# ScalarE takes the first tap of a convolution, and one w_out slice is converted in the fourth stage in place of the second

## The chip, the cores and the metric

One core of a Trainium2 chip runs the kernel. The metric is the device time of one execution in microseconds (us). TensorE (PE) does the matmuls, VectorE (DVE), ScalarE (ACT) and GpSimdE (POOL) the elementwise work, SyncE (SP) issues the transfers. Every engine works off its own queue in order, so an instruction that waits holds up all that stands behind it on that engine.

## The reference, cut to what matters

Causal attention with 2 x 12 heads over 448 tokens, then two feed-forward blocks on 896 tokens of width 768. The second block is where the convolution stands:

```python
h = np.maximum(x @ w_in, 0.0)                 # 768 -> 1024
conv_out = np.zeros_like(h)
for k in range(3):                            # along the tokens
    conv_out += conv_w[k][None, None, :] * hp[:, k:k + S, :]
gate = 1.0 / (1.0 + np.exp(-conv_out))
return (h * gate @ w_out).astype(np.float32)  # 1024 -> 768
```

## The kernel before, in words

Five stages follow each other, and TensorE works in all of them. The first is attention and the receptance products with `w_r`. The second multiplies by `w_k` (slices `wk0` to `wk7`, PSUM tiles `pk`), the third by `w_v` (`wv0` to `wv5`, `pv`), the fourth by `w_in` (`wi0` to `wi7`, `ph`), the fifth by `w_out` (`pout`). Every product of f32 numbers is three matmuls (L64, L65, L66): each operand is split into a high part and a remainder, the low part. L64 and L65 need only the high part of the weight, L66 the low part.

The weights lie in memory as 64-bit floats, and each slice is converted before TensorE can use it. One conversion is a transfer into one of two `wraw` buffers (issued by SP, L122), a ScalarE instruction L100 on the raw words, four VectorE instructions L102, L104, L106 and L108, the split of the high part on ScalarE (L74) and that of the low part on VectorE (L78). The second raw read, L108, frees the `wraw` buffer for the transfer after the next. Tiles `wc` have two buffers; the split weights `whl` have three. The eight slices of `w_out` (`wo0` to `wo7`) are converted ahead of the fifth stage, between the conversions of the other weights: the list `wo_after` says behind which slice each is loaded (two slices later), and calls of `convert_next()` in the loops say where it is converted. Before, three stand in the second stage, three in the third, and two at the end of the fourth.

In the fourth stage, for each of eight slices f and both halves b of the tokens: ScalarE takes the maximum with zero out of PSUM into `hT` (L595), which frees the PSUM bank. VectorE makes the three taps of the convolution in a tile `cv` (L597 multiplies by the first weight, L598 and L599 add the others). ScalarE does the sigmoid (L602), GpSimdE multiplies with `hT` (L603), ScalarE and VectorE split the product into `g` (L74, L78). `hT` has two buffers (one per f), the pool of `cv` three (one per f and b). The PSUM banks are used in a ring of eight, so the first six output tiles `pout` take the banks of `ph4`, `ph5` and `ph6`.

From the second stage on a scheduler of the compiler orders the instructions of each engine by its own estimate of times.

Of the kernel before, what the change touches and what calls it, by code (L numbers as in the profile page):

```python
# [13 lines left out]
AF = mybir.ActivationFunctionType  # L14
ALU = mybir.AluOpType
# [4 lines left out]
def kernel(  # L20
# [18 lines left out]
    nc = tc.nc  # L39
    B, H, S, D = q.shape  # L40
# [9 lines left out]
    NF = DFF // P  # L50
    NE = DM // P
# [8 lines left out]
    def f32(ap):  # L60
        return ap.bitcast(F32)
# [6 lines left out]
    def split_h(eng, out_, in_):  # L68
        if eng == "p":
            nc.gpsimd.tensor_scalar(out_, in_, 1.0, 1.0, ALU.mult, ALU.mult)  # L70
        elif eng == "v":
            nc.vector.tensor_copy(out_, in_)
        else:
            nc.scalar.activation(out_, in_, AF.Copy)  # L74

    def split_l(eng, out_, x, h):
        e = nc.gpsimd if eng == "p" else nc.vector
        e.tensor_tensor(out_, x, f32(h), ALU.subtract)  # L78
# [76 lines left out]
    cw = const.tile([P, 3 * NF], F32, name="cw")  # L155
# [32 lines left out]
    def big(tag, name):  # L188
        return (act if tag in early else act2).tile([P, 2, NT], F32R, tag=tag, name=name)
# [173 lines left out]
    def token_mm(name, w, x, late):  # L363

        n = len(x)
        out_ = [bank(f"{name}_{b}") for b in range(B)]
        for c, b in sorted(((c, b) for b in range(B) for c in range(n)), key=lambda k: (late and k[0] == n - 1, k[1])):
            products(out_[b], w, x, b, n, c)
        return out_
# [8 lines left out]
    units = [(w_r, e, "wr", False) for e in range(NE)] + [(w_k, f, "wk", False) for f in range(NF)]  # L378
    units += [(w_v, e, "wv", False) for e in range(NE)] + [(w_in, f, "wi", False) for f in range(NF)]

    wo_after = [NE + f for f in (1, 3, 5)] + [NE + NF + e for e in (1, 3, 5)] + [len(units) - 1] * 2
    AHEAD = 2
    plan = []
    for u in range(len(units) + AHEAD):
# [24 lines left out]
    def step():  # L409

        if not running:
            running.append(steps_next())
        if next(running[0], running) is running:
            running.clear()

    def convert_next():
        step()
        while running:
            step()

    def take():

        while loaded and not loaded[0][0] and len(ready) <= AHEAD:
            convert_next()
        return ready.pop(0)
# [131 lines left out]
    for f in range(NF):  # L557
        w = take()
        k2.append(big(f"Y{f}", f"k2_{f}"))
        for b, pk in enumerate(token_mm(f"pk{f}", w, xk, f == 0)):  # L560
            t = TOK[b]
            a = mixp.tile([P, S], F32, tag="m", name=f"a{f}_{b}")
            nc.scalar.activation(a, pk, AF.Relu)
            nc.scalar.activation(a, a, AF.Square)
            split_h("s", k2[f][:, 0, t], a)
            split_l("v", k2[f][:, 1, t], a, k2[f][:, 0, t])
        if f in (1, 3, 5):
            convert_next()

    x2 = []  # L570
    for e in range(NE):
# [3 lines left out]
        for b, pv in enumerate(token_mm(f"pv{e}", w, k2, e == 0)):  # L575
            t = TOK[b]
            a = mixp.tile([P, S], F32, tag="m", name=f"xv{e}_{b}")
# [9 lines left out]
    for f in range(NF):  # L587
        w = take()
        g.append(big(f"Y{f}", f"g{f}"))
        hT = hp_.tile([P, B, S + 2], F32, tag="hT", name=f"hT{f}")  # L590
        nc.gpsimd.memset(hT[:, :, 0:S + 2:S + 1], 0.0)
        for b, ph in enumerate(token_mm(f"ph{f}", w, x2, f == 0)):
            t = TOK[b]
            hc = hT[:, b, 1:S + 1]
            nc.scalar.activation(hc, ph, AF.Relu)  # L595
            a = mixp.tile([P, S], F32, tag="m", name=f"cv{f}_{b}")
            nc.vector.tensor_scalar(a, hT[:, b, 0:S], cw[:, f:f + 1], None, ALU.mult)  # L597
            nc.vector.scalar_tensor_tensor(a, hc, cw[:, NF + f:NF + f + 1], a, ALU.mult, ALU.add)  # L598
            nc.vector.scalar_tensor_tensor(  # L599
                a, hT[:, b, 2:S + 2], cw[:, 2 * NF + f:2 * NF + f + 1], a, ALU.mult, ALU.add  # L600
            )
            nc.scalar.activation(a, a, AF.Sigmoid)  # L602
            nc.gpsimd.tensor_tensor(a, a, hc, ALU.mult)  # L603
            split_h("s", g[f][:, 0, t], a)
            split_l("v", g[f][:, 1, t], a, g[f][:, 0, t])
        if f == NF - 1:
            convert_next()
            convert_next()
# [56 lines left out]
```

## Time and profile before

| What | Value |
|---|---|
| Median of 3 runs | 393.79 us (392.92 to 394.78) |
| The profiled execution | 392.92 us, of it 391.1 us span |
| TensorE busy | 382.4 us (98% of the span) |
| VectorE busy | 302.1 us (77%) |
| ScalarE busy | 233.5 us (60%) |
| GpSimdE busy | 113.3 us (29%) |

The page divides the span into forty equal slices. VectorE is at 90% or more in the slices from about 275 to 340 us, which is the fourth stage, and TensorE nearly everywhere. A busy TensorE says little on whether it lost time: its starts do. In the second stage one matmul of 448 columns starts 0.21 us after the one before it, in the third and fourth 0.20 us, and one of 384 columns in the fifth 0.18 us. Where two starts stand farther apart than that, TensorE waited, also where the busy time of two matmuls hides it.

### The profile page before, as it was taken

To read this page: it belongs to the slowest core of one execution; us is meant where nothing else is said; L and a number is where in the kernel's file an instruction comes from. 1 tells how busy PE (TensorE), PEld (TensorE's weight loads), DVE (VectorE), ACT (ScalarE), POOL (GpSimd) and SP (SyncE) were. 2 spreads that over 40 slices of the span, in tenths; PEclk is the share of its full clock that TensorE was granted. 3 is DMA by queue.
4 is the path that set the end of the run, shared out by engine and by line. 5 is a ranking of instruction groups with operands and counts; after the bars stand their busy time and mean duration, and the time that the engine had idled before them with its cause. 6 is when DMAs were issued, how large, how long until landed. Compare 5 with 4: busy or idle time off the path is not lost.

```text
span 391.1 us, 6524 instructions
## 1 busy us (share of the span) xinstructions
PE 382.4 (98%) x2308; PEld 335.9 (86%) x2308; DVE 302.1 (77%) x622; ACT 233.5 (60%) x510; POOL 113.3 (29%) x165
## 2 busy tenths in 40 slices
PE   8999999999999999999998999999999999999996
PEld 7867767767879999898997999999999998999995
DVE  2689999998657886888988898988999999950000
ACT  3698999999426764878776564553545454432111
POOL 1258899999941000000000000000144142320000
PEclk9999999999999999999999999999999999999999
DMA  7546644512220332244554535344522220003111
GB/s 167 119 96 176 158 100 111 153 25 84 80 82 0 117 126 80 92 151 155 168 191 134 189 111 184 92 154 157 164 77 86 80 80 3 1 2 141 40 62 40
DMA packets 60156, 41.34 MB, mean 106 GB/s; under 512 B 34232, under 2 KB 59100, under 8 KB 60124
## 3 DMA queue, kind: packets, MB, share of 16 engines
q1 hardware_dynamic: 60124, 40.93, 34.8%
q8 instruction: 18, 0.29, 0.3%
q14 instruction: 14, 0.11, 0.1%
HBM read 38.17 MB, written 2.75 MB: 105 GB/s over the span
## 4 chain that ended last, share of the span: by engine, by line
PE 53%; DVE 16%; DMA 14%; ACT 7%; issue 7%; POOL 2%; ACTq 0%; SPq 0%; POOLq 0%; DVEq 0%
PE sc L251 7%; PE pp L290 7%; PE po L307 6%; PE pout L64 5%; PE pout L65 5%; PE pout L66 5%; PE pr L64 4%; PE pr L65 4%; PE pr L66 4%; PE warm L447 3%; PE ptrk L231 2%; DMA wk4raw<-in_moe_w_k_dram 1%; POOL cv L603 1%; DVE cv L598 1%; PE ptrq L231 1%
## 5 line engine op out<-in xcount | busy, mean ns | idle before, releaser
L603 POOL TENSOR_TENSOR cv<-cv,hT 128x448 f32<-128x448 f32 x16 | 24.2, 1515 | 204.2 <-ACT cv L602 202.4
L282 POOL TENSOR_SCALAR p<-p,st 112x112 f32<-112x112 f32 (+1 forms) x96 | 56.2, 603 | 21.6 <-DVE st L278 20.9
L270 ACT ACTIVATE p<-s,st 112x112 f32<-112x112 f32 (+3 forms) x96 | 50.5, 533 | 3.7 <-DVE st L262 3.6
L262 DVE CUSTOM_DVE_ANT_0 s<-sc,maskw 112x112 f32<-112x112 f32 (+3 forms) x96 | 39.3, 438 | 5.4 <-PE sc L251 3.0
L251 PE MATMUL sc<-kT,qT 64*112 64x112 f32 (+3 forms) x288 | 30.3, 324 | 0.0
L290 PEld LDWEIGHTS pp<-ident,p 112*112 112x112 f32 x240 | 23.1, 133 | 7.0 <-issue 3.0
L290 PE MATMUL pp<-ident,p 112*112 112x112 f32 x240 | 28.3, 264 | 0.7 <-DVE pt L298 0.7
L630 ACT ACTIVATE osb<-pout 128x384 f32<-128x384 f32 x14 | 6.8, 491 | 32.1 <-PE pout L66 32.0
L307 PE MATMUL po<-pt,rv 112*64 112x448 f32 (+3 forms) x192 | 25.3, 406 | 0.0
L251 PEld LDWEIGHTS sc<-kT,qT 64*112 64x112 f32 x288 | 19.1, 172 | 6.0 <-DVE st L278 0.3
L298 ACT COPY pt<-pp 112x448 f32<-112x448 f32 x36 | 19.1, 533 | 7.9 <-PE pp L290 7.8
L307 PEld LDWEIGHTS po<-pt,rv 112*64 112x64 f32 x192 | 12.7, 136 | 12.2 <-issue 5.5
L343 DVE SCALAR_TENSOR_TENSOR m<-xT,mu,m 128x448 f32<-128x448 f32 x24 | 17.3, 723 | 5.9 <-ACT m L339 3.0
L270 ACT ACTIVATION_READ_ACCUMULATOR p<-s,st 112x1 f32 x96 | 19.3, 201 | 0.0
L74 ACT ACTIVATE g<-cv 128x448 fp32r<-128x448 f32 x16 | 9.2, 576 | 15.7 <-POOL cv L603 15.7
L64 PE MATMUL pout<-wo_t,g 128*128 128x384 f32 x49 | 16.5, 338 | 0.9 <-ACT hT L595 0.9
L65 PE MATMUL pout<-wo_t,g 128*128 128x384 f32 x49 | 16.5, 336 | 0.0
L66 PE MATMUL pout<-wo_t,g 128*128 128x384 f32 x49 | 16.5, 336 | 0.0
L78 POOL TENSOR_TENSOR xr<-m,xr 128x448 fp32r<-128x448 f32 x12 | 16.1, 1341 | 1.0
L602 ACT ACTIVATE cv<-cv 128x448 f32<-128x448 f32 x16 | 9.3, 579 | 10.6 <-DVE cv L599 10.6
L65 PE MATMUL pout<-wo_u,g 128*128 128x384 f32 x42 | 14.1, 336 | 0.0
L64 PE MATMUL pout<-wo_u,g 128*128 128x384 f32 x42 | 14.1, 335 | 0.0
(501 smaller groups left out, 1199.9 us busy)
## 6 DMA issues: line engine op xcount, KB each, us to landing
rq<-in_q_dram SPq DMA_DIRECT2D x24, 112.0 KB, 2.8
rk<-in_k_dram SPq DMA_DIRECT2D x24, 112.0 KB, 2.8
rv<-in_v_dram SPq DMA_DIRECT2D x24, 112.0 KB, 2.8
out_dram<-osb SPq DMA_DIRECT2D x14, 192.0 KB, 1.9
wv0raw<-in_moe_w_v_dram SPq DMA_DIRECT2D x1, 1024.0 KB
wv1raw<-in_moe_w_v_dram SPq DMA_DIRECT2D x1, 1024.0 KB, 4.9
wv2raw<-in_moe_w_v_dram SPq DMA_DIRECT2D x1, 1024.0 KB, 4.9
wv3raw<-in_moe_w_v_dram SPq DMA_DIRECT2D x1, 1024.0 KB, 4.9
```

The costliest lines, as they stand in the source:

```text
L64: nc.tensor.matmul(ps_out, lh, rh, start=first, stop=False)
L65: nc.tensor.matmul(ps_out, lh, rl, start=False, stop=False)
L66: nc.tensor.matmul(ps_out, ll, rh, start=False, stop=last)
L251: nc.tensor.matmul(scs[j][:CP, :w], qT[r, 1 if pi == 2 else 0, c * CP:(c + 1) * CP], kT[r, 1 if pi == 1 else 0, :w], start=pi == 0, stop=p ...
L262: nc.vector.tensor_tensor_reduce(s_sb[:, :w], self.scs[c][j][:CP, :w], maskw[:, S - w:], -SCALE, 3e38, ALU.add, ALU.min, self.st[:, 0, i:i ...
L270: nc.scalar.activation(p, self.s[c, j][:, :w], AF.Exp, bias=self.st[:, 0, i:i + 1], scale=-1.0, accum_out=self.st[:, 1, i:i + 1],)
L282: nc.gpsimd.tensor_scalar(self.p[j, c], self.p[j, c], self.st[:, 2, i:i + 1], 1.0, ALU.mult, ALU.mult)
L290: nc.tensor.transpose(pp[:CP, i * CP:(i + 1) * CP], self.p[j, c][:, kc * CP:(kc + 1) * CP], ident[:CP, :CP])
L298: (nc.vector.tensor_copy if bi in TURN_V else nc.scalar.copy)(pt, self.pp[bi][:CP, :S])
L307: nc.tensor.matmul(self.po[j * D:(j + 1) * D, c0 * CP:S], self.raw["v"][:, kc, j], pt[:, off:off + S - c0 * CP], start=kc == 0, stop=self. ...
L343: nc.vector.scalar_tensor_tensor(m, xT[c][:, b, 1:S + 1], mu[:, a:a + 1], m, ALU.mult, ALU.add)
L603: nc.gpsimd.tensor_tensor(a, a, hc, ALU.mult)
```

## The change

L597, the first tap, is a ScalarE instruction with the weight as its scale in place of a VectorE multiplication. In the second stage `convert_next()` is called after f = 2 and f = 5 in place of 1, 3 and 5; in the fourth it is called once more after f = 3. The list `wo_after` follows: `wo0` is loaded behind `wk4` in place of `wk3`, `wo1` behind `wk7`, and `wo5` behind `wi5`. The third stage converts `wo2` to `wo4` in place of `wo3` to `wo5`.

```diff
-    wo_after = [NE + f for f in (1, 3, 5)] + [NE + NF + e for e in (1, 3, 5)] + [len(units) - 1] * 2
+    wo_after = [NE + f for f in (2, 5)] + [NE + NF + e for e in (1, 3, 5)] + [2 * NE + NF + 3] + [len(units) - 1] * 2
...
-        if f in (1, 3, 5):
+        if f in (2, 5):
             convert_next()
...
             a = mixp.tile([P, S], F32, tag="m", name=f"cv{f}_{b}")
-            nc.vector.tensor_scalar(a, hT[:, b, 0:S], cw[:, f:f + 1], None, ALU.mult)
+            nc.scalar.activation(a, hT[:, b, 0:S], AF.Copy, scale=cw[:, f:f + 1])
...
             split_l("v", g[f][:, 1, t], a, g[f][:, 0, t])
+        if f == 3:
+            convert_next()
         if f == NF - 1:
             convert_next()
             convert_next()
```

On SP, which issues the loads of the weights, this stood in the second stage before:

```order
L122 DMA wk3raw_2394<-in_moe_w_k_dram 128x6x128
L122 DMA wo0raw_2458<-in_moe2_w_out_dram 128x768
L122 DMA wk4raw_2518<-in_moe_w_k_dram 128x6x128
L122 DMA wk5raw_2530<-in_moe_w_k_dram 128x6x128
L122 DMA wo1raw_2590<-in_moe2_w_out_dram 128x768
L122 DMA wk6raw_2650<-in_moe_w_k_dram 128x6x128
L122 DMA wk7raw_2662<-in_moe_w_k_dram 128x6x128
L122 DMA wo2raw_2722<-in_moe2_w_out_dram 128x768
L122 DMA wv0raw_2782<-in_moe_w_v_dram 128x8x128
```

And now, at the same place:

```order
L122 DMA wk3raw_2394<-in_moe_w_k_dram 128x6x128
L122 DMA wk4raw_2458<-in_moe_w_k_dram 128x6x128
L122 DMA wo0raw_2518<-in_moe2_w_out_dram 128x768
L122 DMA wk5raw_2578<-in_moe_w_k_dram 128x6x128
L122 DMA wk6raw_2590<-in_moe_w_k_dram 128x6x128
L122 DMA wk7raw_2650<-in_moe_w_k_dram 128x6x128
L122 DMA wo1raw_2710<-in_moe2_w_out_dram 128x768
L122 DMA wv0raw_2770<-in_moe_w_v_dram 128x8x128
```

`wk4` stands ahead of `wo0`, and one slice fewer stands ahead of `wk6`, `wk7` and `wv0`.

On ScalarE, in the fourth stage around the two tiles `hT6` (`g` are the split products, `wo` slices of w_out), before:

```order
L602 ACTIVATE cv4_1_3727<-cv4_1_3727 128x448
L74 ACTIVATE g4_3676<-cv4_1_3727 128x448
L595 ACTIVATE hT6_3806<-ph6_0_3808 128x448
L595 ACTIVATE hT6_3806<-ph6_1_3809 128x448
L602 ACTIVATE cv5_0_3788<-cv5_0_3788 128x448
```

And now:

```order
L602 ACTIVATE cv4_1_3727<-cv4_1_3727 128x448
L597 ACTIVATE cv5_1_3797<-hT5_3747,cw_81 128x448
L74 ACTIVATE g4_3676<-cv4_1_3727 128x448
L595 ACTIVATE hT6_3806<-ph6_0_3808 128x448
L602 ACTIVATE cv5_0_3788<-cv5_0_3788 128x448
L74 ACTIVATE wo_u5_3357<-wo6c_3925 128x384
L74 ACTIVATE wo6hl_3933<-wo6c_3925 128x384
L74 ACTIVATE g5_3746<-cv5_0_3788 128x448
L597 ACTIVATE cv6_0_3847<-hT6_3806,cw_81 128x448
L602 ACTIVATE cv5_1_3797<-cv5_1_3797 128x448
L595 ACTIVATE hT6_3806<-ph6_1_3809 128x448
```

The taps stand between the others, and the second half of `hT6` now comes six instructions behind the first, after the sigmoid of `cv5_1`.

On VectorE, in the fourth stage ahead of the low part of `wi6`, before:

```order
L599 SCALAR_TENSOR_TENSOR cv2_1_3587<-hT2_3537,cw_81,cv2_1_3587 128x448
L102 TENSOR_SCALAR wi7c_3737<-wi7c_3737 128x768
L78 TENSOR_TENSOR g2_3536<-cv2_0_3578,g2_3536 128x448
L108 SCALAR_TENSOR_TENSOR wi6c_3667<-wi6raw_3595,wi6c_3667 128x768
L597 TENSOR_SCALAR cv3_0_3648<-hT3_3607,cw_81 128x448
L104 TENSOR_SCALAR wi7c_3737<-wi7c_3737 128x768
L597 TENSOR_SCALAR cv3_1_3657<-hT3_3607,cw_81 128x448
L598 SCALAR_TENSOR_TENSOR cv3_0_3648<-hT3_3607,cw_81,cv3_0_3648 128x448
L78 TENSOR_TENSOR g2_3536<-cv2_1_3587,g2_3536 128x448
L106 SCALAR_TENSOR_TENSOR wi7c_3737<-wi7raw_3665,wi7c_3737 128x768
L598 SCALAR_TENSOR_TENSOR cv3_1_3657<-hT3_3607,cw_81,cv3_1_3657 128x448
L78 TENSOR_TENSOR wi6hl_3673<-wi6c_3667,wi6hl_3673 128x768
```

And now:

```order
L599 SCALAR_TENSOR_TENSOR cv3_0_3636<-hT3_3595,cw_81,cv3_0_3636 128x448
L106 SCALAR_TENSOR_TENSOR wi6c_3667<-wi6raw_3653,wi6c_3667 128x768
L598 SCALAR_TENSOR_TENSOR cv3_1_3645<-hT3_3595,cw_81,cv3_1_3645 128x448
L104 TENSOR_SCALAR wi7c_3737<-wi7c_3737 128x768
L78 TENSOR_TENSOR g2_3524<-cv2_1_3575,g2_3524 128x448
L108 SCALAR_TENSOR_TENSOR wi6c_3667<-wi6raw_3653,wi6c_3667 128x768
L599 SCALAR_TENSOR_TENSOR cv3_1_3645<-hT3_3595,cw_81,cv3_1_3645 128x448
L106 SCALAR_TENSOR_TENSOR wi7c_3737<-wi7raw_3665,wi7c_3737 128x768
L78 TENSOR_TENSOR g3_3594<-cv3_0_3636,g3_3594 128x448
L598 SCALAR_TENSOR_TENSOR cv4_0_3718<-hT4_3677,cw_81,cv4_0_3718 128x448
L78 TENSOR_TENSOR wi6hl_3673<-wi6c_3667,wi6hl_3673 128x768
```

No L597 stands there any more, and the convolution is some three tap instructions further when the low part of `wi6` is made. From the first L598 of the stage to `wi6hl` there are 45 VectorE instructions now, among them all of the conversion of `wo5`.

## Rows read from the trace of the kernel before

**Rows 1.** Busy time by engine in the fourth stage and the start of the fifth.

```profile
core 0: us, PE busy (x) PEld busy (x) DVE busy (x) ACT busy (x) POOL busy (x), PEclk, DMA share, GB/s
276.00:349.60 73.60, 72.65 (x375) 68.57 (x374) 71.42 (x100) 35.58 (x63) 25.20 (x22) 1.00 0.20 65
```

**Rows 2.** Timeline of TensorE (start us, us, what) where wk4 begins.

```profile
178.40 0.36 PE L66 MATMUL pk<-xk,wk3hl 128*128 128x448 f32 x1
178.90 0.47 PE L64 MATMUL pk<-xk,wk4hl 128*128 128x448 f32 x1
```

**Rows 3.** Timeline of TensorE where the third stage begins.

```profile
208.72 0.37 PE L66 MATMUL pk<-xk,wk7hl 128*128 128x448 f32 x1
210.07 0.47 PE L64 MATMUL pv<-k,wv0hl 128*128 128x448 f32 x1 [0.99 <-ACT wv0hl L74]
...
210.80 0.37 PE L65 MATMUL pv<-k,wv0hl 128*128 128x448 f32 x1
211.33 0.47 PE L66 MATMUL pv<-k,wv0hl 128*128 128x448 f32 x1 [0.17 <-DVE wv0hl L78]
```

**Rows 4.** Timeline of TensorE in the first output tiles of the fifth stage.

```profile
329.31 0.34 PE L66 MATMUL pout<-wo_t,g 128*128 128x384 f32 x1
330.60 0.44 PE L64 MATMUL pout<-wo_t,g 128*128 128x384 f32 x1 [0.95 <-ACT hT L595]
```

**Rows 5.** Timeline of ScalarE at the same place: both halves of hT6.

```profile
330.02 0.96 ACT L595 ACTIVATE hT<-ph 128x448 f32<-128x448 f32 x2
```

**Rows 6.** Timeline of ScalarE, conversions in the second stage.

```profile
169.72 0.89 ACT L100 ACTIVATE wk4c<-wk4raw 128x768 f32<-128x768 f32 x1 [1.33 <-DMA wk4raw<-in_moe_w_k_dram]
...
196.49 0.89 ACT L100 ACTIVATE wo2c<-wo2raw 128x768 f32<-128x768 f32 x1 [1.70 <-DMA wo2raw<-in_moe_w_out_dram]
...
201.39 1.17 ACT L100 ACTIVATE wv0c<-wv0raw 128x1024 f32<-128x1024 f32 x1 [0.69 <-DMA wv0raw<-in_moe_w_v_dram]
...
208.98 1.04 ACT L74 ACTIVATE wv0hl<-wv0c 128x1024 fp32r<-128x1024 f32 x1
```

**Rows 7.** Lines L597 and L339: durations in ns, minimum/median/maximum, first and last start.

```profile
L597 DVE TENSOR_SCALAR cv<-hT,cw x16: 437/442/1333, 278.2 to 343.3; 128x448 f32<-128x448 f32 x16
L339 ACT ACTIVATE m<-xT,mu x12: 653/659/686, 119.0 to 150.1; 128x448 f32<-128x448 f32 x12
```

**Rows 8.** Timeline of VectorE in the fourth stage up to the low part of wi6.

```profile
307.63 0.55 DVE L104 TENSOR_SCALAR wi7c<-wi7c 128x768 int32<-128x768 int32 x1
308.10 0.44 DVE L597 TENSOR_SCALAR cv<-hT,cw 128x448 f32<-128x448 f32 x1
308.46 0.67 DVE L598 SCALAR_TENSOR_TENSOR cv<-hT,cw,cv 128x448 f32<-128x448 f32 x1
309.06 0.61 DVE L78 TENSOR_TENSOR g<-cv,g 128x448 fp32r<-128x448 f32 x1
309.59 0.94 DVE L106 SCALAR_TENSOR_TENSOR wi7c<-wi7raw,wi7c 128x768 int32<-128x768 int32 x1
310.46 0.67 DVE L598 SCALAR_TENSOR_TENSOR cv<-hT,cw,cv 128x448 f32<-128x448 f32 x1
311.06 0.94 DVE L78 TENSOR_TENSOR wi6hl<-wi6c,wi6hl 128x768 fp32r<-128x768 f32 x1
```

**Rows 9.** Timeline of GpSimdE and VectorE: a multiplication and the instruction beside it.

```profile
313.50 1.17 POOL L603 TENSOR_TENSOR cv<-cv,hT 128x448 f32<-128x448 f32 x1 [6.81 <-ACT cv L602]
...
313.75 1.40 DVE L599 SCALAR_TENSOR_TENSOR cv<-hT,cw,cv 128x448 f32<-128x448 f32 x1
```

**Rows 10.** Timelines of ScalarE and VectorE: the first hT and the first L598.

```profile
276.03 0.53 ACT L595 ACTIVATE hT<-ph 128x448 f32<-128x448 f32 x1
...
279.46 0.68 DVE L598 SCALAR_TENSOR_TENSOR cv<-hT,cw,cv 128x448 f32<-128x448 f32 x1
```

**Rows 11.** Timeline of TensorE: the first matmul of wi6.

```profile
312.78 0.36 PE L64 MATMUL ph<-x,wi6hl 128*128 128x448 f32 x1
```

**Rows 12.** Waits of ScalarE for a transfer, the longest: us in total, times, longest.

```profile
ACT wv5c L100 <- DMA wv5raw<-in_moe_w_v_dram: 4.0, 1, 4.0
```

## The prediction, made before the changed kernel ran

> **What bounds the kernel now.** I read the busy times first, then the starts of TensorE's matmuls, then what released each late start. By busy time TensorE is the bound, at 98% in the table. VectorE is nearly as full in the fourth stage: 71.42 of 73.60 us, with ScalarE at 35.58 and GpSimdE at 25.20 [rows 1]. So work that leaves VectorE there shortens the kernel only by as much as TensorE waits for VectorE. The starts show where it waits after attention. A matmul of 448 columns normally follows its predecessor after 0.20 to 0.21 us, one of 384 columns after 0.18 us, and the first one behind a gap lasts 0.10 us longer. There are four such places, and the change can reach three.
>
> At `wk4` the starts are 178.40 and 178.90, 0.50 us apart: 0.29 us lost, and 0.10 for the slow first one, 0.39 us [rows 2]. At `wv0` the start is 1.35 us late on its predecessor (1.14 lost), later another is 0.53 (0.32 lost), with 0.10 twice: 1.66 us; the releasers are the high part of `wv0` on ScalarE, then the low part on VectorE [rows 3]. In the fifth stage the fifth output tile starts 1.29 us after its predecessor (1.11 lost, 0.10 more): 1.21 us, released by L595 [rows 4], the read of `hT6` that frees the bank [rows 5]. Together 3.26 us. The fourth gap, at `wk2`, lies ahead of the first instruction that the change moves, and stays.
>
> **Second stage: one slice fewer.** `wk4` was late since its raw words were: ScalarE waited 1.33 us for them and read them at 169.72 [rows 6], because `wo0` had taken the `wraw` buffer that came free first. Now `wk4` is loaded ahead of `wo0` and takes that slot on all queues. The swap moves it ahead by a whole slot, and already the 1.33 us of waiting are more than 0.39: the 0.39 us go. `wo0`, behind it, is needed only in the fifth stage. `wk5` has the same number of slices ahead of it as before, so it stays where it was, and it was in time.
>
> `wk6`, `wk7` and `wv0` each move up by one slice. How much that is, the L100 of `wo2` and `wv0` show: 196.49 and 201.39, 4.90 us apart, each after a wait for its transfer [rows 6]. `wv0` now comes right where `wo2` came. Its high part began at 208.98 and took 1.04 us; 4.9 us earlier it is there by 205.1, and its low part, which follows within 1.3 us, by 206.4. TensorE wants the high part at 208.72 + 0.21 - 0.39 = 208.5. Between 2 and 3 us are left, so all 1.66 us go. What would be late next is `wk5`, with no more and no less ahead of it; I leave it at zero.
>
> The third stage has as many conversions as before, in the same places, and TensorE did not wait there. Cost nothing; the cover is TensorE's own matmuls, some 9.7 us for one slice of `w_v`.
>
> **Fourth stage: the tap and wo5.** Sixteen L597 leave VectorE. Each takes 442 ns alone [rows 7], but the next instruction starts 0.36 us after it (308.10 to 308.46) [rows 8], so they free 16 x 0.36 = 5.8 us. `wo5` adds L102 and L104 at 0.47, L106 and L108 at 0.87 and two low parts of about 0.47: 3.6 us. VectorE is relieved by 2.2 us in the stage. ScalarE gets sixteen instructions of the form of L339, a multiplication by a weight per partition of the same 128x448: 659 ns each [rows 7], 10.5 us, and 1.7 us for `wo5`, which makes about 48 of 73.60 us. It has room; whether its order has, decides.
>
> GpSimdE's sixteen multiplications stay, and with them what they cost VectorE: an L599 that stands beside one takes 1.40 in place of 0.67 us [rows 9]. Fifteen instructions in the stage show this, by 0.6 to 1.0 us, whatever their line; I take 0.8.
>
> The critical point is `wi6`, since `wo5` now stands ahead of it. Its low part ended at 312.00 [rows 8], and TensorE began `wi6` at 312.78, wanting the low part two matmuls later, at 313.2 [rows 11]. I count in the clock of the trace of before, because TensorE's arrival and the work that it releases move together. The 45 VectorE instructions from the first L598 to `wi6hl` are 17 of L598 and L599 at 0.60, 7 splits of `g` at 0.53, 4 low parts at 0.87, 8 of L102 and L104 at 0.47, 7 of L106 and L108 at 0.87, and 2 low parts of `wo5` at 0.47 [rows 8]: 28.2 us, and with seven multiplications beside them 33.8. (The same count for the piece of before gives 33.2, the trace 33.8.) The first L598 cannot start before the first `hT`, at 276.03 + 0.53, and the tap, 0.66: 277.2. It stood at 279.46 [rows 10]. With the last conversions of `wi4` now ahead of it I take 278.0. `wi6hl` then ends at 311.8, 1.4 us in time; with the early start 311.0, with the late start and an eighth multiplication 314.1, 0.9 us too late. So a new stall is between 0 and 0.9 us, and I take 0.
>
> The wait at `pout`: the sixth output tile needs the second half of `hT6`, which now stands behind the sigmoid of `cv5_1` on ScalarE. VectorE reaches the end of `cv5_1` 18 instructions after `wi6hl`: 11.2 us by the same prices and 2.4 for three multiplications, so at 325.4. With 0.58 for the sigmoid and 0.53 for L595 the bank is free by 326.7. TensorE wants it at 329.31 + 0.18 + 0.53 = 330.0; before it came at 331.0 [rows 4, 5]. That is 3.3 us in time, and the 1.21 us go. What is late next would be the last slice of `g`, which TensorE wants some 20 us later.
>
> ScalarE's page speaks against the move: the Trainium skill ("ScalarE: Activation LUTs", Rules for kernel authors) sends plain multiplications to VectorE. Per instruction the trace agrees, 659 against 442 ns [rows 7]; by that alone the sixteen would add 16 x 0.22 = 3.5 us of engine time and the rival "ScalarE's queue" below would be the likeliest. The rows weigh more with me, since ScalarE stands idle for half of the stage.
>
> **Sum.** 0.39 + 1.66 + 1.21 = 3.26 us off the profiled execution of 392.92 us (391.1 us span and 1.8 around it): 389.7. That execution is 0.87 us below the median of 393.79. Taken off the median it is 390.5; if part of the spread of the runs is in the waits that go, it is less. I say 390.4.
>
> **The rivals.**
>
> All three waits go (the forecast), 389.7 to 391.0: chance 0.68.
>
> The second stage gains, the fourth does not: `wi6` comes up to 0.9 us late, or the in-order waits between ScalarE and VectorE eat the 1.4 us and `hT6` stays late. For it: the slack is small, and ScalarE's L100 of `wi7` needs raw words whose buffer `wo5` frees late. Against it: the 3.3 us at `hT6`. Only 0.39 + 1.66 = 2.05 us are gained: 391.7; with the 0.9 us on top and the 1.21 us gained 391.4. Chance 0.17.
>
> The change doesn't do what it says in the second stage: `wo1` still stands right ahead of `wv0`, and the scheduler could let the freed time pass, so that `wv0` stays late. For it: the scheduler, not the source, sets the order. Against it: the queue of the loads, where one slice less stands ahead. Gain 0.39 + 1.21 = 1.60: 392.2. Chance 0.08.
>
> ScalarE's queue, the slower one: every L100 that waits for its transfer now stands ahead of taps, where before VectorE made the taps itself. Three loads come in that part of the stage (`wo5`, `wi6`, `wi7`). If each held ScalarE as long as the longest wait in this trace, 4.0 us [rows 12], the second half of `hT6` would come 12 us later, at 338.7, 8.7 us after it is wanted; the waits at `wi6` and `wi7` are part of these. 389.7 + 8.7 + 0.87 = 399.3. It decides from 3.3 + 3.3 = 6.6 us of such waits, where the gain is used up; against it speaks that VectorE's queue of half-ready work covers 1 or 2 us of each, and that these loads find a free buffer long ahead. Chance 0.07.
>
> **How the numbers follow.** About 0.5%, 2.0 us, is what a measurement of this kernel can tell from no change, so faster means below 391.8. The forecast lies there but for its upper tail (0.65 of 0.68), the second case in about 0.10 of its 0.17: faster 0.75. The rest of these and the third case are the same: 0.18. Slower 0.07. The range goes from 389.1, the full sum on a run like the profiled one and 0.6 us of spread, to 392.4, which holds the third case; it leaves out the slower case and some of the tails.
>
> **What would show it.** Right: after attention only the gap at `wk2` is left between TensorE's starts; `wv0hl` on ScalarE ends more than 2 us before its first matmul; `wi6hl` ends up to 2 us before it is needed, and the second half of `hT6` 3 us before. VectorE's share in the fourth stage falls by some 2 us. Wrong: a start of `wi6`, `wi7` or `pout` that is released by VectorE or by L595, or ScalarE waiting for transfers of `wo5` to `wi7` with VectorE idle behind it.

## The result, and the profile after

The changed kernel takes 389.80 us (median of 4 runs, 389.40 to 390.37), the kernel before beside it 393.94 us (4 runs, 392.92 to 394.78). The ratio is 0.9904, with a 95% interval of 0.9877 to 0.9930: faster, by 0.6 us more than forecast and inside the range. The profiled execution took 389.52 us, of it 387.7 us span, which is 3.4 us less than before. Measured once more, beside other runs of the kernel before, the ratio was 0.9929 (0.9912 to 0.9946).

The first lines of the page after:

```profile
span 387.7 us, 6519 instructions
...
PE 380.2 (98%) x2308; PEld 335.5 (87%) x2308; DVE 295.2 (76%) x606; ACT 243.2 (63%) x526; POOL 111.3 (29%) x165
```

TensorE's waits after, the whole list (us in total, times, longest):

```profile
PE warm L447 <- POOL ident masks.py:199: 1.8, 1, 1.8
PE ph L66 <- DVE wi6hl L78: 1.0, 1, 1.0
PE pp L290 <- DVE pt L298: 0.8, 1, 0.8
```

The releasers of [rows 3, 4] are gone from it, and a new one stands there: the low part of `wi6`. The first and the last line belong to the start and to attention and were there before.

The timeline of TensorE after, at `wk4`, `wv0` and `wi6`:

```profile
177.88 0.36 PE L66 MATMUL pk<-xk,wk3hl 128*128 128x448 f32 x1
178.08 0.37 PE L64 MATMUL pk<-xk,wk4hl 128*128 128x448 f32 x1
...
207.07 0.36 PE L66 MATMUL pk<-xk,wk7hl 128*128 128x448 f32 x1
207.27 0.36 PE L64 MATMUL pv<-k,wv0hl 128*128 128x448 f32 x1
...
309.42 0.36 PE L64 MATMUL ph<-x,wi6hl 128*128 128x448 f32 x1
309.62 0.36 PE L65 MATMUL ph<-x,wi6hl 128*128 128x448 f32 x1
310.96 0.47 PE L66 MATMUL ph<-x,wi6hl 128*128 128x448 f32 x1 [0.98 <-DVE wi6hl L78]
```

`wk4` and `wv0` now follow 0.20 us behind their predecessors, where 0.50 and 1.35 us stood [rows 2, 3]. At `wi6` the third matmul starts 1.34 us behind the second: 1.14 lost and 0.10 for the slow first one, 1.24 us that were not there before.

The span's 3.4 us, stretch by stretch from TensorE's starts in both traces (one profiled execution each):

| Stretch | before | after | difference, us |
|---|---|---|---|
| start of the span to `wk0` (ahead of all that changed) | 148.74 | 148.22 | -0.52 |
| `wk3` to `wk4` (gap [rows 2]) | 7.60 | 7.29 | -0.31 |
| `wk4` to `wv0` (first gap [rows 3], a small one in `wk4`, and the pace, below) | 31.17 | 29.19 | -1.98 |
| `wv0` to `wi0` (second gap [rows 3]) | 58.93 | 58.37 | -0.56 |
| `wi0` to `wi6` | 43.78 | 43.78 | 0.00 |
| `wi6` to the first `pout` (the new gap) | 14.59 | 15.83 | +1.24 |
| first to last `pout` (gap [rows 4]) | 59.56 | 58.24 | -1.32 |

`wk0` to `wk3` and what follows the last `pout` take the same time in both.

### The profile page after: what moved, and what is told of

Its sections match the earlier page's. It is cut to its first block, busy times and chain, and to the rows that moved or that the text cites. A ratio compares the mean times of both kernels' runs of the same rounds, so it can differ in the third digit from the quotient of the medians.

```text
span 387.7 us, 6519 instructions
## 1 busy us (share of the span) xinstructions
PE 380.2 (98%) x2308; PEld 335.5 (87%) x2308; DVE 295.2 (76%) x606; ACT 243.2 (63%) x526; POOL 111.3 (29%) x165
## 4 chain that ended last, share of the span: by engine, by line
PE 59%; DVE 23%; DMA 10%; ACT 4%; issue 3%; POOL 0%; ACTq 0%; SPq 0%; POOLq 0%
PE sc L251 7%; PE pp L290 7%; PE po L307 6%; PE pout L65 5%; PE pout L66 5%; PE pout L64 5%; PE pr L64 4%; PE pr L66 4%; PE pr L65 4%; PE warm L447 3%; DVE cv L598 2%; PE ptrk L231 2%; DMA wv0raw<-in_moe_w_v_dram 2%; PE ptrq L231 1%; PE ph L66 1%
## 5 line engine op out<-in xcount | busy, mean ns | idle before, releaser
L603 POOL TENSOR_TENSOR cv<-cv,hT 128x448 f32<-128x448 f32 x16 | 22.1, 1384 | 198.4 <-ACT cv L602 198.4
L598 DVE SCALAR_TENSOR_TENSOR cv<-hT,cw,cv 128x448 f32<-128x448 f32 x16 | 15.7, 982 | 0.7 <-ACT cv L597 0.7
```

## The experiments

The kernels were measured in three sets, each beside the kernel before on the same chip. The medians of before were 393.41 us in the first set, 392.89 in the second and 392.88 in the third. The second set ran on another chip than the third; since their medians of before agree, their times are set side by side below.

| Kernel | set | median, us (runs) | ratio, 95% interval | TensorE's gaps of 0.1 us or more in its profile, `wk2` left out |
|---|---|---|---|---|
| e1_tap | 1 | 393.26 (10) | 0.9985, 0.9952 to 1.0018 | `wv0`, twice |
| e2_move | 1 | 391.79 (10) | 0.9957, 0.9934 to 0.9981 | `wi6`, twice |
| e3_third | 1 | 389.01 (4) | 0.9871, 0.9835 to 0.9907 | none |
| e4_swap | 1 | 392.56 (10) | 0.9966, 0.9937 to 0.9996 | `wv0` twice, `pout` |
| e5_gap | 2 | 391.59 (12) | 0.9956, 0.9931 to 0.9980 | `wv0`, put back |
| e6_third_tapv | 2 | 390.85 (10) | 0.9946, 0.9923 to 0.9968 | `pout` |
| e8_end | 2 | 388.26 (4) | 0.9891, 0.9852 to 0.9929 | none |
| e7_wk2 | 2 | 391.70 (10) | 0.9973, 0.9948 to 0.9997 | `wk3`, `wi6` (`wk2` gone) |
| after_again | 3 | 390.07 (6) | 0.9929, 0.9912 to 0.9946 | `wi6` |
| e3_again | 3 | 388.92 (5) | 0.9897, 0.9881 to 0.9913 | `wi7` |
| e8_again | 3 | 388.88 (4) | 0.9896, 0.9879 to 0.9913 | none |

**The tap alone, in the kernel before.**

```diff
-            nc.vector.tensor_scalar(a, hT[:, b, 0:S], cw[:, f:f + 1], None, ALU.mult)
+            nc.scalar.activation(a, hT[:, b, 0:S], AF.Copy, scale=cw[:, f:f + 1])
```

> The kernel before with the tap alone: L597 is a ScalarE instruction, the slices of w_out stay where they were (three in the second stage). Theory (the time follows the gaps between TensorE's starts, and VectorE's load makes the gap in the fourth stage): the gaps at wk4 (0.39 us) and wv0 (1.66 us) stay, the one at pout (1.21 us) goes, and wi6 has none, since no wo5 stands ahead of it: ratio to before about 0.997. Rival (ScalarE's queue delays the convolution, so the changed kernel's new gap at wi6 comes from the tap): a gap of about 1 us at wi6 here too, ratio 1.000.

The wait at `pout` is gone, and no wait stands in the fourth stage. The low part of `wi6` starts at 308.90 and lasts 0.94 us; TensorE wants it at 315.6. So the tap removes the gap of [rows 4] and by itself makes no new one. The median can't be told from before's; the interval holds the expected 0.997 as well as 1. The profiled execution, at 394.39 us, was even longer than that of before. The timeline of TensorE in it, and its windows behind the gap (the columns of [rows 1]), show where it lost time:

```profile
207.03 0.36 PE L66 MATMUL pk<-xk,wk7hl 128*128 128x448 f32 x1
209.00 0.47 PE L64 MATMUL pv<-k,wv0hl 128*128 128x448 f32 x1 [1.61 <-ACT wv0hl L74]
...
210.26 0.74 PE L66 MATMUL pv<-k,wv0hl 128*128 128x448 f32 x1 [0.18 <-DVE wv0hl L78]
...
213.70 0.36 PE L66 MATMUL pv<-k,wv0hl 128*128 128x448 f32 x1
```

```profile
210.20:213.60 3.40, 3.34 (x9) 2.99 (x10) 3.40 (x6) 2.02 (x4) 0.00 (x0) 0.50 0.25 82
214.00:220.00 6.00, 6.00 (x31) 5.45 (x30) 4.53 (x6) 2.00 (x3) 0.00 (x0) 1.00 0.62 193
```

The wait at `wv0` stayed (1.77 us lost, then 0.34), and behind it the granted clock was at 0.50, the level of 1.2 GHz, for 3.4 us: ten starts, from 210.26 to 213.70, took 3.44 us where 2.03 is usual, so 1.4 us were lost once more. Ahead of it TensorE had waited twice, 1.61 and 0.18 us; in the second row it is back at 1.00, 2.4 GHz. From there to the end of `wi7` the starts were 206.7 ns apart where e3_third has 202.7, over 576 matmuls 2.3 us. So the unchanged gap cost more in this execution than in the profiled one of before.

**The moved conversions alone, the tap back on VectorE.**

```diff
-            nc.scalar.activation(a, hT[:, b, 0:S], AF.Copy, scale=cw[:, f:f + 1])
+            nc.vector.tensor_scalar(a, hT[:, b, 0:S], cw[:, f:f + 1], None, ALU.mult)
```

> The changed kernel with the tap back on VectorE: only the slices of w_out are moved. Theory (wo5 costs VectorE 3.6 us ahead of wi6, and the tap pays for it): the second stage gains as in the changed kernel, 0.39 + 1.66 us and the faster pace of wk4 to wk7 (0.6 us), together 2.6 us; wi6 comes at least 2 us too late and pout later still, 3 to 5 us of gaps in the fourth stage against 1.21 before: ratio 0.998 to 1.006. Rival (wi6 is late in the changed kernel for ScalarE's queue, not for VectorE's load): no gap at wi6, only pout's 1.21 us: ratio 0.993.

```profile
312.16 0.47 PE L64 MATMUL ph<-x,wi6hl 128*128 128x448 f32 x1 [0.91 <-ACT wi6hl L74]
...
313.77 0.33 PE L65 MATMUL pout<-wo_t,g 128*128 128x384 f32 x1
315.57 0.47 PE L66 MATMUL ph<-x,wi6hl 128*128 128x448 f32 x1 [1.46 <-DVE wi6hl L78]
```

The timeline of TensorE shows two gaps at `wi6`, 1.08 and 1.62 us, 2.9 with the slow firsts; `wk4`, `wv0` and `pout` have none. So the moved slices alone remove the gaps of [rows 2, 3]. They also make the one at `wi6`, and the tap cuts it from 2.9 to 1.24 us. (In this kernel the scheduler put five matmuls of `pout`, 0.9 us, ahead of the late one; without them the gap would have been longer by as much.) The time is shorter than expected: 0.9957 against 0.998 to 1.006, with 2.9 us of gaps against 3 to 5. No wait is left at `pout`, where TensorE now comes later by what it lost at `wi6`; with the tap on VectorE and `wi6` in time it is back (e6_third_tapv, below).

**wo5 in the third stage, all else as changed.** No conversion of `w_out` stands ahead of `wi6` in the fourth stage.

```diff
-    wo_after = [NE + f for f in (2, 5)] + [NE + NF + e for e in (1, 3, 5)] + [2 * NE + NF + 3] + [len(units) - 1] * 2
+    wo_after = [NE + f for f in (2, 5)] + [NE + NF + e for e in (1, 2, 3, 5)] + [len(units) - 1] * 2
...
-        if e in (1, 3, 5):
+        if e in (1, 2, 3, 5):
...
-        if f == 3:
-            convert_next()
```

> The changed kernel with wo5 converted in the third stage (calls after e = 1, 2, 3 and 5), where TensorE's next slice is ready 5 to 13 us early; the fourth stage converts two slices at its end as before. Theory: the gap of 1.23 us at wi6 goes and none comes in its place: 1.2 us less than the changed kernel, ratio to before 0.987. Rival (the pipeline of conversions only shifts, wi6 stays late since its raw words or the third stage become late): the gap stays or moves to wi0 to wi5, ratio 0.990 or more.

Timeline of VectorE, then of TensorE in this kernel:

```profile
306.17 0.94 DVE L78 TENSOR_TENSOR wi6hl<-wi6c,wi6hl 128x768 fp32r<-128x768 f32 x1
```

```profile
310.24 0.36 PE L66 MATMUL ph<-x,wi6hl 128*128 128x448 f32 x1
```

The low part of `wi6` is there at 307.11, 3.1 us before it is wanted. TensorE has no gap after attention but the old one at `wk2` and 0.08 us at `wi7`, and the third stage takes the additional slice without one. The place of `wo5` is the cause of the new gap.

**One swap alone, in the kernel before:** `wk4` is loaded ahead of `wo0`.

```diff
-    wo_after = [NE + f for f in (1, 3, 5)] + [NE + NF + e for e in (1, 3, 5)] + [len(units) - 1] * 2
+    wo_after = [NE + f for f in (2, 3, 5)] + [NE + NF + e for e in (1, 3, 5)] + [len(units) - 1] * 2
...
-        if f in (1, 3, 5):
+        if f in (2, 3, 5):
```

> The kernel before with wo0 converted behind f = 2 in place of f = 1, so that wk4 is loaded ahead of it; nothing else is changed. It removes the gap at wk4 alone. Theory (the slower pace of TensorE in wk4 to wk7, 206.7 against 202.7 ns from start to start, belongs to the gap at wk4): gap and pace go together, 0.39 + 0.6 us, ratio 0.9975. Rival (the pace belongs to the three slices of w_out in the second stage, their transfers or conversions): 206.7 ns stay from wk4 on, 0.39 us at most, ratio 0.999.

ScalarE in e4_swap, then in e1_tap, where the order of the loads is that of before:

```profile
172.26 0.83 ACT L74 ACTIVATE wk4hl<-wk4c 128x768 fp32r<-128x768 f32 x1
```

```profile
176.88 0.84 ACT L74 ACTIVATE wk4hl<-wk4c 128x768 fp32r<-128x768 f32 x1
```

In e1_tap the high part of `wk4` is complete 0.28 us before TensorE begins `wk4` at 178.00: it was on the edge. ScalarE and VectorE work through the second stage in the same order in both kernels, so the gap of [rows 2] comes in one execution and not in another. With the swap it is complete at 173.09, 5.8 us early. The gaps at `wv0` (1.38 and 0.34 us) and `pout` (1.04) stay. So the swap makes `wk4` early and leaves `wv0` late; for `wv0` it takes the slice fewer, and the prediction was right to give the two waits different causes. Besides, the starts in `wk4` to `wk7` are 202.7 ns apart here, and in e1_tap too, where three slices stand in the second stage but the gap at `wk4` did not come; in the kernel before they are 206.7 apart. So the slower pace goes with the gap and not with the slices.

**The gap at wv0 put back into e3_third.** The high part of `wv0` is written four times over.

```diff
-            split_h(he, t[:, 0, :z], c[:, o:o + z])
+            for _ in range(4 if name == "wv0" else 1):
+                split_h(he, t[:, 0, :z], c[:, o:o + z])
```

> e3_third, with the high part of wv0 written four times over in place of once, so that wv0 is late again and TensorE waits some 1 to 2 us at the start of the third stage; nothing else is changed. Theory (a gap costs more than its length: behind it TensorE may go on at 206.7 in place of 202.7 ns from start to start until the next gap, which over the 576 matmuls of the third and fourth stage is 2.3 us, and the clock may fall for some us): the runs spread over 2.5 us or more, where those of e3_third lay within 0.8, and some are 3 to 5 us above it; ratio 0.993 to 1.000. Rival (the gap costs its length alone): 1 to 2 us above e3_third in every run, spread 1 us, ratio 0.990 to 0.992.

```profile
207.19 0.37 PE L66 MATMUL pk<-xk,wk7hl 128*128 128x448 f32 x1
209.12 0.47 PE L64 MATMUL pv<-k,wv0hl 128*128 128x448 f32 x1 [1.57 <-ACT wv0hl L74]
```

The profile has a gap of 1.73 us, 1.93 with the slow firsts, behind which the pace stays at 202.7 ns and the clock at 1.00. That execution took 390.47 us, 1.0 us above the profiled one of e3_again, which has a gap of its own at `wi7`, and 1.8 above that of e3_third, which has none of 0.1 us. The median lies higher, at 391.59 against 388.92 of e3_again, 2.67 us, and its runs spread over 4.1 us against 1.1. So the gap cost its length in the profiled execution, and in most of the others more. Four of the twelve have a mean granted clock of 0.996, where those of e3_third and e3_again have 0.998 or more; what the rest lost beyond the gap is not shown, and the slower pace seen in e1_tap is a candidate.

**The tap back on VectorE, in e3_third.**

```diff
-            nc.scalar.activation(a, hT[:, b, 0:S], AF.Copy, scale=cw[:, f:f + 1])
+            nc.vector.tensor_scalar(a, hT[:, b, 0:S], cw[:, f:f + 1], None, ALU.mult)
```

> e3_third with the tap back on VectorE: the slices of w_out stand 2, 4 and 2, and the fourth stage is that of the kernel before. Theory (the tap is what removes the gap at pout, the moved slices what removes those of the second stage): no gap in the second and third stage, and one of about 1.2 us at pout, released by the read of hT6: 1.2 us above e3_third, ratio 0.990. Rival (the earlier conversions alone let the fourth stage be in time): no gap at pout, ratio 0.987, and the tap was worth nothing.

```profile
327.12 0.34 PE L66 MATMUL pout<-wo_t,g 128*128 128x384 f32 x1
328.53 0.44 PE L64 MATMUL pout<-wo_t,g 128*128 128x384 f32 x1 [1.08 <-ACT hT L595]
```

Only the gap of [rows 4] is back: 1.23 us and 0.10. It is 390.85 against 388.92 us of e3_again (ratios 0.9946 and 0.9897), so the tap on ScalarE is worth some 1.9 us here, of which the profile shows 1.33. The rule of the Trainium skill ("ScalarE: Activation LUTs", Rules for kernel authors) that plain multiplications go to VectorE would give the opposite. It holds per instruction, 442 against 670 ns here, and an engine with room may still be the better place.

**wo5 at the end of the fourth stage,** loaded behind `wi7` and converted with `wo6` and `wo7`.

```diff
-    wo_after = [NE + f for f in (2, 5)] + [NE + NF + e for e in (1, 3, 5)] + [2 * NE + NF + 3] + [len(units) - 1] * 2
+    wo_after = [NE + f for f in (2, 5)] + [NE + NF + e for e in (1, 3, 5)] + [len(units) - 1] * 3
...
-        if f == 3:
-            convert_next()
         if f == NF - 1:
+            convert_next()
             convert_next()
             convert_next()
```

> The changed kernel with wo5 loaded behind wi7 and converted at the end of the fourth stage, with wo6 and wo7: it stays in that stage, but no longer ahead of wi6. Theory (the gap of 1.23 us at wi6 comes from where wo5 stands in VectorE's queue): gap gone, the later wo5 is covered since the fifth stage needs it 16 us after its start, ratio 0.987 like e3_third. Rival (the fourth stage holds too much work whatever the order): a gap of about 1 us at wi6, at pout or at a late g or wo slice, ratio 0.990 or more.

Timeline of VectorE, then of TensorE in this kernel:

```profile
302.25 1.74 DVE L78 TENSOR_TENSOR wi6hl<-wi6c,wi6hl 128x768 fp32r<-128x768 f32 x1
```

```profile
309.62 0.37 PE L66 MATMUL ph<-x,wi6hl 128*128 128x448 f32 x1
```

The low part is there at 303.99, 5.6 us early, and no gap came at the end of the stage either. This is the shortest median.

**The gap at wk2, tried on top of e3_third** with one more conversion ahead of the second stage.

```diff
+    convert_next()
     manual.close()
```

> e3_third with one more conversion, wk2, started before the second stage's loop in place of within it. It aims at the last gap, 0.65 us at wk2. Theory (wk2 is late since its conversion is queued behind the first results of the second stage): the gap shrinks or goes, up to 0.65 us less than e3_third, ratio 0.9855 to 0.987. Rival (wk2 is late for its buffer or ScalarE's first wait, which stay): no difference to e3_third, 0.987.

A miss: 0.9973, where both theory and rival had 0.987 or less. The gap at `wk2` went, but the slice in front made `wk3` late, and the kernel is 2.78 us slower than e3_again. The timeline of TensorE at the new gap, at the first matmuls of `wv3` and `wv4`, which stand 48 matmuls apart, and at a small gap in `wi6`:

```profile
172.22 0.47 PE L66 MATMUL pk<-xk,wk3hl 128*128 128x448 f32 x1 [0.23 <-DVE wk3hl L78]
...
238.45 0.37 PE L64 MATMUL pv<-k,wv3hl 128*128 128x448 f32 x1
...
248.37 0.37 PE L64 MATMUL pv<-k,wv4hl 128*128 128x448 f32 x1
...
313.06 0.37 PE L65 MATMUL ph<-x,wi6hl 128*128 128x448 f32 x1
313.51 0.47 PE L66 MATMUL ph<-x,wi6hl 128*128 128x448 f32 x1
```

The gap itself is 0.38 us and 0.10. From it to the one in `wi6` the starts are 206.7 ns apart (9.92 us for the 48), and then 202.7 again. Some 680 matmuls stand in these 141 us, 2.7 us more at 4 ns each.

**The three versions side by side.**

> The changed kernel once more, beside e3_third and e8_end on the same chip. Theory (the gap at wi6 is what is left, 1.23 us and at times a slower pace behind it): 1 to 2 us slower than the other two, ratio to before 0.990 to 0.994. Rival (the versions differ by less than the chips do): all three within 0.5 us.

> e3_third once more, for the comparison with the changed kernel on one chip: no gap but the one at wk2, ratio 0.987 to 0.990.

> e8_end once more, for the same comparison: no gap but the one at wk2, the same ratio as e3_again to 0.002. Rival (the third stage is the worse or better place for wo5): they differ by more.

The changed kernel is at 390.07 us, and both versions without `wo5` ahead of `wi6` are faster, by 1.15 and 1.19 us; the gap at `wi6` in the first profile was 1.24. The times of e3 and e8 can't be told apart, but the profiles can: e3_again has an unexpected wait at `wi7`, 0.89 us and 0.10, and e8_again none. VectorE in e3_again, TensorE in it, then VectorE in e8_again:

```profile
316.42 1.73 DVE L78 TENSOR_TENSOR wi7hl<-wi7c,wi7hl 128x768 fp32r<-128x768 f32 x1
```

```profile
318.21 0.47 PE L66 MATMUL ph<-x,wi7hl 128*128 128x448 f32 x1 [0.73 <-DVE wi7hl L78]
```

```profile
310.55 1.73 DVE L78 TENSOR_TENSOR wi7hl<-wi7c,wi7hl 128x768 fp32r<-128x768 f32 x1
```

With `wo5` in the third stage the low part of `wi7` is on the edge: it cost TensorE 0.08 us in the profile of e3_third and 0.99 in that of e3_again. With `wo5` at the end of the fourth it is complete at 312.28, 5.1 us before its matmul at 317.42. TensorE in after_again:

```profile
310.68 0.36 PE L65 MATMUL ph<-x,wi6hl 128*128 128x448 f32 x1
312.18 0.47 PE L66 MATMUL ph<-x,wi6hl 128*128 128x448 f32 x1 [1.15 <-DVE wi6hl L78]
```

So the gap at `wi6` came again: 1.30 us, and 0.10 for the slow first matmul, beside 1.14 and 0.10 in the first profile.

## Why the prediction was right, and where it was not

**The three waits: right, each by its own cause.** `wk4` (0.39 us), `wv0` (1.66) and `pout` (1.21) all went, 3.26 us as summed. e4_swap and e2_move show the second stage's two causes, e1_tap shows that the tap removes the wait at `pout`, and e6_third_tapv that the wait stays without the tap where `wi6` is in time. ScalarE after, at `wv0` and at the second half of `hT6`, then TensorE at the sixth output tile:

```profile
203.69 1.06 ACT L74 ACTIVATE wv0hl<-wv0c 128x1024 fp32r<-128x1024 f32 x1 [0.54 <-DVE wv0c L108]
...
325.05 0.52 ACT L595 ACTIVATE hT<-ph 128x448 f32<-128x448 f32 x1
```

```profile
327.87 0.34 PE L64 MATMUL pout<-wo_t,g 128*128 128x384 f32 x1
```

The high part of `wv0` is complete at 204.75, as forecast by 205.1, and the low part at 206.13 (by 206.4). TensorE began at 207.27 and not at 208.5, since it had gained time ahead of that too (below), so the high part was 2.5 us early, where the forecast's own times leave 3.4; it had said 2 to 3. The second half of `hT6` is read by 325.57, where before both halves were done at 330.98 [rows 5]. That is 2.3 us before the sixth output tile, where 3.3 were forecast (the forecast's terms add up to 326.5 and not 326.7 for the end of the read, so to 3.5). The walk from `wi6hl` to there was right, 13.6 us forecast and measured; it started 2.5 us late, and TensorE, held up at `wi6`, came 1.24 us later itself. The margin covered the rest.

**The tap's price: right.** Line L597 after, as [rows 7]:

```profile
L597 ACT ACTIVATE cv<-hT,cw x16: 652/670/676, 273.2 to 335.0; 128x448 f32<-128x448 f32 x16
```

670 ns against 659 from the neighbouring line.

**The bound at wi6: wrong, the term that failed.** It was 0 to 0.9 us, taken at 0; measured 1.24. The prediction had named such a start of `wi6`, released by VectorE, as a sign that it was wrong. In the clock of the trace after (3.36 us earlier at `wi6`) the walk said: first L598 at 274.6, 276.1 at the latest, low part complete at 308.4. The timeline of ScalarE, then of VectorE:

```profile
271.84 0.90 ACT L100 ACTIVATE wi4c<-wi4raw 128x768 f32<-128x768 f32 x1 [3.16 <-DMA wi4raw<-in_moe_w_in_dram]
```

```profile
266.11 0.95 DVE L108 SCALAR_TENSOR_TENSOR wi2c<-wi2raw,wi2c 128x768 int32<-128x768 int32 x1
...
272.77 0.56 DVE L102 TENSOR_SCALAR wi4c<-wi4c 128x768 f32<-128x768 f32 x1 [1.56 <-ACT wi4c L100]
...
275.83 0.68 DVE L598 SCALAR_TENSOR_TENSOR cv<-hT,cw,cv 128x448 f32<-128x448 f32 x1
...
308.46 1.57 DVE L598 SCALAR_TENSOR_TENSOR cv<-hT,cw,cv 128x448 f32<-128x448 f32 x1
309.96 0.94 DVE L78 TENSOR_TENSOR wi6hl<-wi6c,wi6hl 128x768 fp32r<-128x768 f32 x1
```

Two things were mis-sized. First, VectorE had run ahead until it had nothing to convert. The buffer for `wi4` came free with the L108 of `wi2`, which ended at 267.06. ScalarE then waited 3.16 us for the transfer and VectorE 1.56 us for ScalarE, so the first L598 came at 275.83, 1.2 us after the value taken. The walk had the last conversions of `wi4` ahead of it, but not the wait for their transfer: its early value came from `hT` and the tap, its late one from the kernel before. The rival on ScalarE's queue had looked for such waits at `wo5`, `wi6` and `wi7` only. Second, the 45 instructions took 35.07 us and not 33.8, since eight of them stood beside a multiplication of GpSimdE and not seven, the last just ahead of `wi6hl` (1.57 in place of 0.68). Together 2.5 us: out of 1.4 us in time came a low part complete at 310.90, where TensorE wanted it at about 309.8.

The upper end, 0.9 us, had the late start (276.1) and an eighth multiplication in it. The start kept within it by 0.3 us, but the 45 instructions took 0.5 us more than the 34.6 that eight stretches at 0.8 us give, and the slow first matmul, 0.10, was not counted: 0.3 us beyond the bound.

**Missing from the sum.** The pace: `wk4` to `wk7` had 206.7 ns between starts before and 202.7 after, over 144 matmuls 0.6 us; the prediction read "0.20 to 0.21" and did not ask why. A second, small wait in `wk4` before, which is gone as well:

```profile
179.62 0.37 PE L65 MATMUL pk<-xk,wk4hl 128*128 128x448 f32 x1
179.89 0.47 PE L66 MATMUL pk<-xk,wk4hl 128*128 128x448 f32 x1
```

The first use of the low part starts 0.07 us late and lasts 0.10 longer, 0.17 us. And 0.52 us came from ahead of any changed instruction, which the change can't be credited with: over the traces of all the kernels here that stretch takes 148.0 to 149.9 us. So the sum reads 3.26 - 1.24 + 0.6 + 0.17 + 0.5 = 3.3 of the 3.4 us. That the time agreed so well with the forecast is in part luck, since the missed loss and the missed gains cancel. The forecast was 0.6 us above the measured median; without the new gap it would have been some 1.8 us above, since e3_again and e8_again are 1.15 and 1.19 us shorter than after_again.

**The rivals.** The second, with `wi6` late on top, was half right: that stall came, larger than its 0.9 us, but `hT6` was early. The third falls, since `wo1` still stood right ahead of `wv0` and did no harm. The slow one falls too, as to its size: ScalarE waited 3.16 us for `wi4`, and of that 1.56 us reached VectorE and 1.2 the convolution.

**VectorE's share.** The windows of the fourth stage, as [rows 1]:

```profile
274.00:347.60 73.60, 72.62 (x377) 68.62 (x376) 64.54 (x84) 44.43 (x78) 23.03 (x22) 1.00 0.18 60
```

VectorE fell by 6.9 us, not by 2.2. The sixteen L597 were 9.4 us in that window, stretches included (588 ns each on the mean, where the prediction had 360), and `wo5` brought 4.0 us: 5.4 us less. The rest isn't resolved; conversions of `wi2` to `wi4` lie at the window's edge, `wi3` inside it before and ahead of it after. The share told nothing of the one wait that is left, which is set by what stands ahead of `wi6hl`.

## What to carry to other kernels

Cost a moved piece of work by what stands between it and the next operand that the busiest engine wants on the same in-order queue: work that is needed late goes behind the last such operand, not where the engine's share looks lowest. When an engine is relieved, look for what it will run into (here a buffer whose transfer had not landed), since the slack that was given back does not all arrive. A short wait of TensorE can cost more than its length (in e1_tap a slower clock and a slower pace followed one), so count gaps and their places first, and after that the engines' shares.

## What the runs showed of the hardware

**Two paces of TensorE.** A matmul of 448 columns follows its predecessor after 202.7 or 206.7 ns, both at a granted clock of 1.00. The first matmuls of `wk6` and `wk7`, which stand 36 matmuls apart, before and after:

```profile
194.04 0.37 PE L64 MATMUL pk<-xk,wk6hl 128*128 128x448 f32 x1
...
201.48 0.37 PE L64 MATMUL pk<-xk,wk7hl 128*128 128x448 f32 x1
```

```profile
192.68 0.36 PE L64 MATMUL pk<-xk,wk6hl 128*128 128x448 f32 x1
...
199.98 0.36 PE L64 MATMUL pk<-xk,wk7hl 128*128 128x448 f32 x1
```

These are 7.44 and 7.30 us. In the traces read for it the pace changes at a gap and is kept to the next one, or to the end of the matmuls of that size. It was 206.7 ns from `wk4` to `wv0` before, from `wv0` to the end of `wi7` in e1_tap, from `wk3` to `wi6` in e7_wk2, from `wi6` on in after_again. Behind other gaps, that of e5_gap among them, it stays at 202.7. What decides it at a gap was not found.

**The granted clock behind a gap.** Beside the row of e1_tap, each execution gives a mean granted clock. Over the 65 executions of the kernel before in the three sets, the 40 with a mean of 0.999 or more have a median of 392.78 us, the 8 at 0.997 to 0.998 one of 393.08, the 14 at 0.995 to 0.996 one of 394.16, and the 3 at 0.993 to 0.994 one of 395.92. In the 27 executions of the changed kernel, e3 and e8 it never was below 0.997, against 17 of the 65. So part of what the change brings seems to lie in executions in which the clock drops before and no longer does after; that it drops behind the gap at `wv0` is shown for one execution of e1_tap alone.

**Stretched instructions of VectorE.** The Trainium skill ("SBUF — State Buffer", SBUF: two separate sides) says that VectorE and GpSimdE share a pair of ports that one of them holds for a whole instruction. The rows agree:

```profile
307.96 1.59 POOL L603 TENSOR_TENSOR cv<-cv,hT 128x448 f32<-128x448 f32 x1 [3.78 <-ACT cv L602]
```

This multiplication of GpSimdE ran from 307.96 to 309.55, and the L598 shown above beside it, of 0.68 us alone, began at 308.46 and ended at 310.03, 0.48 us behind it. At 281.10 another ran for 1.52 us, to 282.62, and the L598 beside it ended at 283.10, 0.48 us behind it again.
